# Block-sparse attention with a gated projection: the second half's keys in twelve smaller loads, and two more row loads in place of copies

## The chip, the cores and the metric

The kernel runs on one core of one Trainium2 chip. The metric is the time of one execution on the device in microseconds (us); the figure for a kernel is the median of its runs. Lower is better.

## The reference, cut to what matters

```python
# q, k, v: 4 batches, 8 heads, 768 rows, 64 columns; sampled_blocks: 24 x 3 block numbers
scores = scale * np.matmul(q, k.transpose(0, 1, 3, 2))
mask = np.abs(blk_i - blk_j) <= 1                      # blocks of 32 rows: own block and neighbours
mask = mask | (blk_i == 0) | (blk_j == 0) | (blk_i == 23) | (blk_j == 23)
for qb in range(24):
    for kb in sampled_blocks[qb]:                      # three sampled key blocks a query block
        mask[qb*32:(qb+1)*32, kb*32:(kb+1)*32] = True
attn = softmax(np.where(mask, scores, -1e9))
x = matmul(attn, v)                                    # heads joined: 4 x 768 x 512
gate_pre = causal depthwise convolution of x, 5 taps
out = (sigmoid(gate_pre) * (x @ w_val)) @ w_out
```

## The kernel before, in words

The four batches are worked off in two phases of two batches each (phase 0: batches 0 and 1, phase 1: batches 2 and 3). In a phase there are 22 ordinary parts, one for each query block `i` from 1 to 22, which serve both batches and all heads at once, and two global parts (query blocks 0 and 23 of one batch each, against all 24 key blocks), so 24 parts a phase. A global part takes two steps of the main loop (line 804), an ordinary part one. A step issues for its own part the score matmuls (tile `sc`, or `s` for a global part), for the part of the step before the transposes of the softmax weights (`pt`, evicted as `ptr`), for the part two steps before the products with the values (`av`). Around them it places pieces of the gate, the splitting of fp32 numbers into two parts, and the two projections (`vp`, `op`). Two tables of digits say how many such pieces each half step gets (lines 54 to 67). The order on each engine is fixed when the program is built.

The ordinary parts go in pairs (`PAIRS`: blocks 1 and 2, 3 and 4, and so on). Pair number `p` has the blocks 2p+1 and 2p+2.

**Keys.** The tile `keys` (`k` in the profile) holds one phase's keys of both batches, 24 blocks. `load_all_keys` (line 287) brings them in by `KEY_PARTS`; `K_AT` (line 34) names the part of the 48 with whose loads each piece is issued on SyncE's queue (SP). The phase 1 keys overwrite those of phase 0 block by block. For each pair `copy_keys` gathers the blocks that the pair needs into `kg`, a ring of two buffers of a pair each: the fixed blocks always by copies on GpSimd (POOL), and the three sampled blocks of a part by POOL copies out of `keys` (phase 0, blocks up to 18) or by SP loads from memory (all later ones, 128 KB each).

**Values.** A part needs the rows of its sampled blocks (`vb`, an indirect load of 128 rows which POOL issues, ring of three) and 128 rows for the fixed blocks: 64 end rows (blocks 0 and 23) and 64 own rows of the pair. For a pair of phase 0 with an even number `p`, the own rows lie in the upper half of a tile `vn` already, and the end rows are brought into its lower half; with an odd one the own rows are brought to the end rows in the tile `va`. They are brought by a POOL copy (`owns.append(copy_rows)`), or, for pairs from `ROWS_FROM` on, by a load of 260 KB on SP:

```python
            if f == 0 and pr.p >= ROWS_FROM:
                at, row = (2 * BLK, 2 * BLK * (pr.p + 1)) if own else (0, 0)
                sp.dma_start(pr.va[at : at + 2 * BLK]..., v[row : row + 2 * BLK, :])
            else:
                owns.append(copy_rows)
```

**Queues.** SP issues nearly all transfers in one order: queries (`qc`, ring of five), weights (`wst`), keys, sampled keys, rows and results. A transfer whose buffer is still read holds up those behind it. Each transfer also takes one of eight completion semaphores in turn, so SP waits for the transfer eight before it. POOL issues the indirect loads in order with its copies.

Of the kernel before, what the change touches and what calls it, by code (L numbers as in the profile page):

```python
# [17 lines left out]
BLK, NB, NR = 32, 24, 3  # L18
# [8 lines left out]
F, E = 2, B // 2  # L27
# [2 lines left out]
VRING = 3  # L30
GLOB_AT = ((0, 0), (12, 18))
V_AT = ((0, 0, 1, 1, 1, 1, 2, 2, 3, 4, 4, 5), (0, 0, 3, 12, 12, 16))
KEY_PARTS = (((0, 0, 8), (0, 8, 16), (0, 16, 24), (1, 0, 8), (1, 8, 16), (1, 16, 24)), tuple((E, a, a + 4) for a in range(0, NB, 4)))
K_AT = (0, 0, 0, 1, 1, 1, 22, 24, 24, 24, 27, 29)
LAG_T, LAG_V, LAG_X = 1, 2, 3
WEIGHTS_AT = (1, 2, 5, 6, 7, 8, 8, 9, 10, 11, 11, 12, 13, 14, 18, 19)
DECODE_LAG = 2
# [2 lines left out]
VALUES_FROM = 4  # L40
INDEX_AT = 3
SPARE_UNTIL = 18
ROWS_FROM = 4
WARM = 13
EVICTED = (4,)

# [25 lines left out]
def attention_moe(ctx, tc, qb, kb, v, sampled, w_val, conv_w, w_out, ident_in, slot_in, out):  # L72
# [210 lines left out]
    def load_all_keys():  # L283
        for f in range(F):
            for e, a, z in KEY_PARTS[f]:
                some = slice(e, e + 1) if e < E else slice(0, E)
# [59 lines left out]
    def load_keys(pr):  # L346
# [6 lines left out]
        if not pr.glob:  # L353
            for place, reg in block_numbers(pr, SP):
                sp.dma_start(pr.kg[:, 1 + pr.j, place], kb[:, f, :, bass.ds(reg, 1)].rearrange("p e o x -> p e (o x)"))
        for _ in range(K_AT.count(parts.index(pr))):
            next(loading_keys)
# [38 lines left out]
    def load_values(pr):  # L396
# [5 lines left out]
        if pr.j == 0:  # L402
# [17 lines left out]

            if f == 0 and pr.p >= ROWS_FROM:
                at, row = (2 * BLK, 2 * BLK * (pr.p + 1)) if own else (0, 0)
# [508 lines left out]
```

## Time and profile before

| | us |
|---|---|
| median of 3 runs | 353.4 (352.46 to 356.05) |
| profiled execution, its own time | 353.03 |
| span of the profile (first to last instruction) | 351.3 |
| TensorE matmul busy | 329.3 (94%) |
| VectorE busy | 274.9 (78%) |
| ScalarE busy | 226.3 (64%) |
| GpSimd busy | 118.7 (34%) |
| moved by DMA | 67.74 MB, mean 193 GB/s |

The profile is of one execution. PE is TensorE's matmuls, PEld its weight loads, DVE VectorE, ACT ScalarE, POOL GpSimd, SP SyncE's queue. Nearly all instructions pass through one recording helper, so they have line 90 (`L90`) and are told apart by their tiles. The idle time in brackets behind an instruction is that of its engine just before it, with what ended it; "issue" there means that the engine waited for nothing that the profile shows. The DMA share is the mean busy share of 16 DMA engines; it can go above 1, since the times of packets overlap.

### The profile page before, as it was taken

What the parts mean: (1) busy time and instruction counts of PE and PEld (TensorE: products, weight loads), DVE (VectorE), ACT (ScalarE), POOL (GpSimd) and SP (SyncE); (2) the same over time, 40 slices, a digit from 0 to 9 for tenths busy, and PEclk for the clock granted to TensorE, in tenths of its full rate; (3) what the DMA queues carried; (4) which work ended last, traced back from release to release, by engine and by line L of the source; (5) the groups of instructions that cost most, each with busy time, mean ns of one, the idle gap of its engine ahead of it and who ended that gap; (6) DMA issues with size and microseconds to landing.
All of it is one profiled execution on the core that took longest, in us unless ns stands there. A gap on an engine that the chain in (4) does not pass through costs nothing.

```text
span 351.3 us, 15356 instructions
## 1 busy us (share of the span) xinstructions
PE 329.3 (94%) x6522; PEld 258.0 (73%) x6522; DVE 274.9 (78%) x644; ACT 226.3 (64%) x505; POOL 118.7 (34%) x186
## 2 busy tenths in 40 slices
PE   8787989989867999999999999999999999999995
PEld 7465756655545887797788777887778878989894
DVE  0664878999999789759997984768987599989440
ACT  2365877687896757756785674758766786564421
POOL 1647788877643304414431222321242100000000
PEclk9899999999999999999999999999999999999999
DMA  6958587876999999774888567538663011020202
GB/s 219 395 194 261 174 266 256 276 251 170 277 283 294 385 247 305 250 225 154 273 228 279 165 205 219 173 107 251 200 204 95 12 58 62 30 90 2 90 0 90
DMA packets 47603, 67.74 MB, mean 193 GB/s; under 512 B 4400, under 2 KB 31536, under 8 KB 47536
## 3 DMA queue, kind: packets, MB, share of 16 engines
q1 hardware_dynamic: 40624, 43.10, 39.5%
q0 software_dynamic: 6336, 23.43, 21.1%
q8 instruction: 51, 0.84, 1.0%
q10 hardware_dynamic: 576, 0.24, 0.2%
q14 instruction: 16, 0.13, 0.1%
HBM read 60.46 MB, written 6.29 MB: 190 GB/s over the span
## 4 chain that ended last, share of the span: by engine, by line
PE 75%; DVE 14%; ACT 7%; issue 3%; POOL 0%; ACTq 0%; POOLq 0%; DVEq 0%
PE op L90 19%; PE vp L90 19%; PE av L90 12%; PE pt L90 11%; PE sc L90 9%; DVE mx L90 5%; PE s L90 3%; DVE words L90 3%; ACT ptr L90 3%; PE idle L90 2%; ACT pe L90 2%; DVE wst L90 2%; DVE xT L90 1%; DVE x L90 1%; DVE wv L90 1%
## 5 line engine op out<-in xcount | busy, mean ns | idle before, releaser
L90 ACT ACTIVATE pe<-sc,mx 128x256 f32<-128x256 f32 x176 | 69.1, 475 | 36.6 <-DVE mx L90 36.2
L90 POOL DMA_INDIRECT vb<-in_v,idx x44 | 44.4, 1010 | 142.7 <-PE av L90 120.8
L90 DVE SCALAR_TENSOR_TENSOR th<-xT,cw,th 128x384 f32<-128x384 f32 x128 | 79.7, 652 | 1.5 <-ACT th L90 1.5
L90 DVE TENSOR_REDUCE mx<-sc 128x2 f32<-128x512 f32 x88 | 56.3, 679 | 21.2 <-PE sc L90 17.5
L90 ACT COPY ptr<-pt 128x512 f32<-128x512 f32 x108 | 61.3, 606 | 9.3 <-PE pt L90 8.0
L90 POOL COPY kg<-k 128x256 f32 (+1 forms) x99 | 55.2, 596 | 7.5 <-PE sc L90 7.0
L90 PE MATMUL sc<-kg,qc 64*32 64x256 f32 x1408 | 53.3, 382 | 2.3 <-issue 1.1
L90 PE MATMUL op<-wo,yh 128*128 128x512 f32 x192 | 53.3, 399 | 0.0
L90 PE MATMUL pt<-ident,pe 128*128 128x128 f32 x352 | 50.4, 279 | 1.8 <-issue 1.8
L90 PE MATMUL vp<-xh,wv 128*128 128x384 f32 x256 | 51.1, 341 | 0.0
L90 PEld LDWEIGHTS vp<-xh,wv 128*128 128x128 f32 x256 | 44.3, 188 | 0.3
L90 PEld LDWEIGHTS pt<-ident,pe 128*128 128x128 f32 x352 | 38.5, 140 | 7.3 <-issue 1.9
L90 PEld LDWEIGHTS op<-wo,yh 128*128 128x128 f32 x192 | 35.3, 188 | 7.3
L90 PEld LDWEIGHTS sc<-kg,qc 64*32 64x32 f32 x1408 | 22.8, 106 | 21.2 <-issue 9.6
L90 ACT CAST yh<-y 128x384 fp32r<-128x384 f32 x32 | 16.8, 524 | 23.0 <-DVE y L90 23.0
L90 PE MATMUL av<-vb,ptr 128*32 128x65 f32 x1408 | 28.8, 220 | 2.4 <-issue 2.4
L90 PE MATMUL op<-wo,yl 128*128 128x512 f32 x96 | 30.9, 403 | 0.0
L90 PEld LDWEIGHTS av<-vn,ptr 128*32 128x32 f32 x1216 | 19.2, 109 | 14.6 <-ACT ptr L90 7.5
L90 PEld LDWEIGHTS av<-va,ptr 128*32 128x32 f32 x960 | 15.6, 109 | 17.2 <-ACT ptr L90 9.5
L90 PE MATMUL av<-vn,ptr 128*32 128x65 f32 x1216 | 24.5, 222 | 3.6 <-ACT ptr L90 1.7
L90 PE MATMUL vp<-xl,wv 128*128 128x384 f32 x128 | 27.7, 338 | 0.0
L90 DVE TENSOR_TENSOR yl<-y,yh 128x384 fp32r<-128x384 f32 x32 | 18.3, 572 | 11.4 <-ACT yh L90 11.1
(74 smaller groups left out, 421.8 us busy)
## 6 DMA issues: line engine op xcount, KB each, us to landing
kg<-in_k SPq DMA_DIRECT2D x80, 128.0 KB
qc<-in_q SPq DMA_DIRECT2D x48, 128.0 KB
k<-in_k SPq DMA_DIRECT2D x12, 512.0 KB
out<-ot SPq DMA_DIRECT2D x23, 256.0 KB
vn<-in_v SPq DMA_DIRECT2D x16, 260.0 KB
vn<-in_v SPq DMA_DIRECT2D x6, 520.0 KB
va<-in_v SPq DMA_DIRECT2D x8, 260.0 KB
wst<-in_w_val SPq DMA_DIRECT2D x8, 256.0 KB
```

The source lines that it names most:

```text
L90: made = getattr(self.eng, name)(*args, **kwargs)
```

## The change

Two edits of constants. The phase 1 keys come in twelve loads of two blocks (256 KB) in place of six of four blocks (512 KB), one each with the parts 21 to 32, where it was 22, three with 24, then 27 and 29. And `ROWS_FROM` goes from 4 to 2, so pairs 2 and 3 of phase 0 also load their 64 rows on SP, and POOL no longer copies them.

```diff
-KEY_PARTS = ((...), tuple((E, a, a + 4) for a in range(0, NB, 4)))
-K_AT = (0, 0, 0, 1, 1, 1, 22, 24, 24, 24, 27, 29)
+KEY_PARTS = ((...), tuple((E, a, a + 2) for a in range(0, NB, 2)))
+K_AT = (0, 0, 0, 1, 1, 1, 21, 22, 23, 24, 25, 26, 27, 28, 29, 30, 31, 32)
-ROWS_FROM = 4
+ROWS_FROM = 2
```

POOL, pair 3 of phase 0, around the indirect load of its first part (`vb_1186`, which is `vb_1187` in the change). Before:

```order
L90 DMA vb_1186<-in_v,idx_109 128x1040
L90 COPY va1_114<-vn_141 64x1040
L90 COPY kg0_111<-k_110 128x512
L90 COPY kg0_111<-k_110 128x2x256
L335 TENSOR_LOAD sm_103
```

The change:

```order
L90 DMA vb_1187<-in_v,idx_109 128x1040
L90 COPY kg0_111<-k_110 128x512
L90 COPY kg0_111<-k_110 128x2x256
L335 TENSOR_LOAD sm_103
```

The copy is gone and the key copies stand one place further ahead; the copy `vn_133<-vn_131` of pair 2 goes in the same way. No instruction moves on PE, DVE or ACT.

SP at the same stretch (`wst` are pieces of the weights, `qc` queries). Before:

```order
L90 DMA wst_907<-in_w_val 128x512
L90 DMA qc_1002<-in_q 128x256
L90 DMA wst_907<-in_w_val 128x512
L90 DMA wst_1006<-in_w_val 128x512
L90 DMA qc_1109<-in_q 128x256
L90 DMA wst_1006<-in_w_val 128x512
L90 DMA qc_1206<-in_q 128x256
```

The change:

```order
L90 DMA wst_907<-in_w_val 128x512
L90 DMA vn_133<-in_v 64x1040
L90 DMA qc_1002<-in_q 128x256
L90 DMA wst_907<-in_w_val 128x512
L90 DMA wst_1006<-in_w_val 128x512
L90 DMA qc_1109<-in_q 128x256
L90 DMA wst_1006<-in_w_val 128x512
L90 DMA va1_114<-in_v 64x1040
L90 DMA qc_1206<-in_q 128x256
```

Two row loads come in, the first ahead of `qc_1002`, the second ahead of `qc_1206`.

SP at the burst of key loads, with part 24 (`kg1_112` are its sampled keys). Before:

```order
L90 DMA kg1_112<-in_k 128x2x128
L90 DMA k_110<-in_k 128x2x512 x3
L90 DMA qc_2576<-in_q 128x256
L90 DMA vn_2578<-in_v 128x1040
```

The change:

```order
L90 DMA kg1_112<-in_k 128x2x128
L90 DMA k_110<-in_k 128x2x256
L90 DMA qc_2576<-in_q 128x256
L90 DMA vn_2578<-in_v 128x1040
```

Of 1,536 KB in a row 256 KB are left here. One load of 256 KB now stands behind the sampled keys of each of the parts 21 to 32.

## Rows read from the trace of the kernel before

**Rows 1.** The page: engines, the instruction queue, the chain by engine.

```profile
PE 329.3 (94%) x6522; PEld 258.0 (73%) x6522; DVE 274.9 (78%) x644; ACT 226.3 (64%) x505; POOL 118.7 (34%) x186
...
q8 instruction: 51, 0.84, 1.0%
...
PE 75%; DVE 14%; ACT 7%; issue 3%; POOL 0%; ACTq 0%; POOLq 0%; DVEq 0%
```

**Rows 2.** Stretches: window, length, busy by engine (instructions), clock, DMA share, GB/s.

```profile
40.00:46.00 6.00, 5.88 (x200) 4.50 (x200) 5.63 (x15) 5.01 (x14) 3.65 (x6) 1.00 0.60 171
46.00:52.00 6.00, 4.77 (x172) 3.14 (x156) 3.76 (x9) 4.19 (x10) 5.35 (x9) 1.00 0.82 274
...
97.00:103.00 6.00, 4.14 (x135) 2.80 (x119) 6.00 (x16) 5.13 (x14) 2.92 (x3) 1.00 1.09 270
103.00:109.00 6.00, 4.22 (x159) 2.97 (x147) 6.00 (x15) 5.28 (x13) 2.70 (x3) 1.00 0.97 279
...
115.00:121.00 6.00, 6.00 (x70) 5.21 (x72) 3.81 (x11) 5.21 (x12) 2.48 (x3) 1.00 1.05 395
121.00:127.00 6.00, 6.00 (x97) 5.87 (x97) 5.04 (x12) 4.12 (x10) 0.96 (x1) 1.00 1.13 243
```

**Rows 3.** Waits over the span: engine and tile, releaser, us, times, longest.

```profile
POOL vb L90 <- PE av L90: 120.8, 36, 11.4
...
PEld sc L90 <- POOL kg L90: 0.9, 3, 0.4
```

**Rows 4.** Waits of SP's queue over the span.

```profile
SPq L90 <- DMA k<-in_k: 7.0, 7, 1.5
```

**Rows 5.** Timeline of POOL: start, length, instruction, idle before it.

```profile
45.89 1.06 POOL L90 COPY vn<-vn 64x1040 f32<-64x1040 f32 x1
...
54.96 1.04 POOL L90 COPY va<-vn 64x1040 f32<-64x1040 f32 x1
...
116.33 1.17 POOL L90 COPY kg<-k 128x512 f32<-128x512 f32 x2
```

**Rows 6.** Timeline of SP's queue.

```profile
40.68 1.04 SPq L90 DMA_DIRECT2D wst<-in_w_val  x1
...
51.65 0.33 SPq L90 DMA_DIRECT2D qc<-in_q  x1
...
95.85 1.02 SPq L90 DMA_DIRECT2D qc<-in_q  x1
...
100.68 0.38 SPq L90 DMA_DIRECT2D k<-in_k  x1
...
110.28 2.52 SPq L90 DMA_DIRECT2D k<-in_k  x3
```

**Rows 7.** Timeline of PE, two stretches in which it pauses.

```profile
48.65 0.33 PE L90 MATMUL av<-va,ptr 128*32 128x65 f32 x9 [0.95 <-issue]
...
51.41 0.67 PE L90 MATMUL av<-va,ptr 128*32 128x65 f32 x32
...
53.17 0.50 PE L90 MATMUL av<-vb,ptr 128*32 128x65 f32 x18 [0.87 <-issue]
...
56.07 0.32 PE L90 MATMUL av<-vn,ptr 128*32 128x65 f32 x8
...
100.75 0.55 PE L90 MATMUL av<-vb,ptr 128*32 128x65 f32 x23 [1.57 <-issue]
...
106.30 1.09 PE L90 MATMUL pt<-ident,pe 128*128 128x128 f32 x8 [1.77 <-issue]
...
112.61 1.05 PE L90 MATMUL sc<-kg,qc 64*32 64x256 f32 x19 [0.89 <-issue]
```

**Rows 8.** Timelines: first uses of pair 3's rows (PE) and block 11's queries (ACT).

```profile
63.08 0.96 PE L90 MATMUL av<-va,ptr 128*32 128x65 f32 x32
...
64.61 0.41 ACT L90 ACTIVATE qc<-qc 128x256 f32<-128x256 f32 x1
```

**Rows 9.** The tile vb: its indirect loads, issue to landing.

```profile
DMA to landing us min/median/max: 5.0/5.8/8.0
```

More of the change, by code (lines that the diff above doesn't have):

```diff
@@ L32 @@
 V_AT = ((0, 0, 1, 1, 1, 1, 2, 2, 3, 4, 4, 5), (0, 0, 3, 12, 12, 16))
-KEY_PARTS = (((0, 0, 8), (0, 8, 16), (0, 16, 24), (1, 0, 8), (1, 8, 16), (1, 16, 24)), tuple((E, a, a + 4) for a in range(0, NB, 4)))
-K_AT = (0, 0, 0, 1, 1, 1, 22, 24, 24, 24, 27, 29)
+KEY_PARTS = (((0, 0, 8), (0, 8, 16), (0, 16, 24), (1, 0, 8), (1, 8, 16), (1, 16, 24)), tuple((E, a, a + 2) for a in range(0, NB, 2)))
+K_AT = (0, 0, 0, 1, 1, 1, 21, 22, 23, 24, 25, 26, 27, 28, 29, 30, 31, 32)
 LAG_T, LAG_V, LAG_X = 1, 2, 3
```

## The prediction

> **What bounds the kernel now.** I read first the page's engine line and its chain by engine: PE's matmuls are busy for 94% of the span, and 75% of the chain that ended last is PE's, 14% VectorE's, none POOL's [rows 1]. So a change of loads and POOL copies can only move the time where PE, or VectorE in its stead, waits for what it changes. Where that can be is in the table of stretches. From 115 us on PE is busy all of each stretch (6.00 of 6.00), while VectorE and POOL have gaps; there a transfer that comes earlier is worth nothing. Before, PE has gaps (4.14 and 4.22 of 6.00 in the two stretches from 97 to 109 us), and VectorE has none in these [rows 2]. The list of waits then says who would feel a faster POOL: POOL waits 120.8 us for PE to free the ring of `vb`, and the other way round PE's weight loads wait 0.9 us in all for POOL's key copies [rows 3]. Last, PE's timeline shows what its gaps are. The long ones are not waits for a tile at all: five pauses of 0.95, 0.87, 1.57, 1.77 and 0.89 us, marked as "issue", four of them in the middle of a group of equal matmuls whose first members had run [rows 7]. The page has a DMA queue for instructions, 51 packets and 0.84 MB [rows 1]; divided by PE's 13,044 instructions that is 64 bytes each, so this queue feeds PE, some 256 instructions a packet. I read the pauses as PE running out of instructions. The first two fall in or beside a stretch in which the DMA share has risen from 0.60 to 0.82, the others where it is 0.97 and more [rows 2]. So the load on the DMA engines is the one way in which this change can reach PE, and it matters from about 40 to 113 us.
>
> **The rows, part by part.** The change removes two POOL copies, 1.06 and 1.04 us [rows 5], and with them 2.1 us of POOL's time. Behind them wait the key copies of pairs 2 and 3, and behind those PE's score matmuls; that wait is at most the 0.9 us of the list, which three places share [rows 3]. I take nothing: from there to 109 us VectorE is full [rows 2] and its work is not shortened. Bounds: 0 and -0.5 us.
>
> In their place SP issues two loads of 260 KB. The first stands behind a piece of the weights issued by 41.7 us; its rows are first read at 56.07 us [rows 6, 7]. No row gives the landing time of such a load, but an indirect one of twice its size lands in 5.0 to 8.0 us [rows 9]. Even with 8.0 us it is there by 50. The second overwrites rows that pair 1 reads at 51.41 us for 0.67 us [rows 7], so it can only go out at 52.1 us, and SP waits there. Behind it are the queries of block 11, issued at 51.65 us so far [rows 6], and pieces of the weights. The queries go out some 0.5 us behind the load, at 52.6 us, and with 8.0 us land at 60.6; ScalarE first reads them at 64.61 us. The rows themselves land by 60.1, and PE reads them at 63.08 us [rows 8]. So both waits are covered, by 4.0 and 3.0 us. If that cover were gone (a landing of over 11 us), PE would wait for the rows next.
>
> The Trainium skill, "SBUF — State Buffer", section "SBUF: two separate sides", has VectorE and GpSimd lock one another out for a whole instruction on the port pair that they share, so by it each copy could hold up one VectorE instruction by its whole length and the change would give back up to 2.1 us. The list of waits above shows no VectorE work released by these copies, and the sum by the trace stays at 0.
>
> **The keys, part by part.** The bytes stay the same, 3 MB; SP issues six transfers more. One of 512 KB took SP 0.38 us, three in a row 2.52 us [rows 6], so 0.4 to 0.8 us each, 2.4 to 5 us spread over the steps from 95 us on. SP waits in that time for buffers that PE frees; I take 0. The first piece goes out behind the sampled keys of part 21, at about 96 us, the second where a load of 512 KB stood, at 100.7 us, the fourth at 110.3 us where now 1,536 KB go out [rows 6]. POOL's copy for the first pair of phase 1 starts at 116.33 us [rows 5], 15 us after the second piece, which it needs. Each later pair needs one piece more, while one goes out with every part, two for each pair. So no copy should wait for its keys.
>
> What is left is the effect on PE's pauses. Until 110 us there are now three pieces, 768 KB, where 512 KB stood: 256 KB more, which at the 279 GB/s of that stretch [rows 2] are 0.92 us of transfer. Behind 110 us there are 1,280 KB less, but from there PE has one pause left, 0.89 us, and its packet was probably under way by then. Bounds for the three pauses from 100 to 113 us: all gone, -4.23 us; each longer by the whole transfer, +2.8 us. I take +0.2 us: the two pauses ahead of the burst a little longer, the third shorter by half.
>
> The Trainium skill, "Runtime: NRT & Kernel Launch", section "Instruction fetch mechanics", says that the sequencer fetches the next 16 KiB of instructions while it runs the current ones and that the cost of crossing a block is mostly hidden. By that rule the term would be 0 whatever the DMA engines do. The five pauses speak against it here, as far as my reading of them holds.
>
> **The sum.** Against the profiled execution's own time of 353.03 us: rows 0, keys on SP 0, pauses +0.2, which makes 353.2 us. The median of the runs shown is 353.4, 0.4 us above that execution; the runs spread over 3.6 us, 1%, so less than 1% can't be told from no change. I forecast no change.
>
> **The rivals.**
>
> 1. Faster: PE's instruction packets get through. For it: three pauses, 4.23 us, lie in the stretch with the highest DMA share, and the largest burst of the kernel, 1,536 KB in one go, is taken apart. Against it: two of the pauses lie ahead of the burst, and ahead of it the change adds bytes. If all three go, 353.4 - 4.2 = 349.2 us; with two of them, about 350.2.
>
> 2. Slower, in the same place: the stretch from 95 to 110 us gets 256 KB more while its DMA share is 0.97 to 1.09 already. Each pause then grows by up to 0.92 us, and the two at 48 and 53 us by as much, since the first row load falls ahead of them: five times 0.92 is 4.6 us, 358 us; the three late ones alone 356.2. It decides from the point at which the share in 97 to 109 us stays above about 1.1. Against it: at 115 to 121 us the engines moved 395 GB/s at a share of 1.05, so 270 and 279 GB/s are not all that they can do [rows 2].
>
> 3. Slower: the smaller key loads are moved at the worse of two rates. At 243 GB/s, the rate from 121 to 127 us, 3.1 MB take 12.8 us, at 395 GB/s 8.0 [rows 2]. If these 4.8 us came on the path, 358.2 us. But only SP has waited for keys until now, 7.0 us in all [rows 4], and the cover is 15 us, so a copy on POOL would have to come that late before it decides. The Trainium skill, "DMA: Bandwidth & Descriptors", section "Measured (HBM→SBUF, 128 partitions, SWDGE, issued from GpSimd)", asks for transfers of 1 MiB and more, which speaks against splitting; its figures are for another path, and no run here shows a load alone.
>
> 4. The change does little because its parts never were on the path: that is the forecast itself. That it doesn't do what it says I rule out by the order of instructions: both copies are gone, the burst is one load.
>
> **How the numbers follow.** The forecast gets 0.74, rival 1 0.13, rival 2 0.10, rival 3 0.03. The forecast's own range is 352.2 to 354.5 us, from the bounds of the small terms and half of one pause either way. Rivals 1 and 2 reach over 1% (below 349.9 or above 356.9) only when most of their pauses go or grow. Faster by over 1%: 0.08 from rival 1 and 0.02 for what I don't see. Slower by over 1%: 0.06 from rival 2, 0.03 from rival 3 and 0.01 for what I don't see. Within 1%: 0.80. The range runs from 350.0, two pauses gone and a little more, to 355.8 us, the three late pauses longer by most of their bound.
>
> **What would show it.** In the profile after: no POOL copy of 64 rows at 46 and 55 us and key copies 1 us earlier there, with PE's first 115 us no shorter than by 0.5 us; a row load on SP at about 52 us with the queries right behind it; key loads of one each from about 96 us to 170 us; PE full from 115 us on. I would be wrong if PE or POOL waited for `k`, `va` or `vn`, or if the sum of the pauses marked "issue" between 45 and 113 us, 6.05 us now [rows 7], changed by more than 2 us.

## The result: 0.6 to 1.5% slower, and the profile after

The changed kernel takes 355.67 us (median of 5 runs, 354.46 to 359.62); the kernel before took 353.4 beside it (median of 5). The ratio is 1.0102, with an interval of 1.0056 to 1.0149. Each ratio here is taken over the undisturbed executions and is not the plain quotient of two medians, which is 1.0064 in this case. The forecast was 353.2 us and no change. The time is inside the range, at its upper end, but the forecast's case is wrong: the change costs about 1%.

The profiled execution of after took 354.46 us, 1.4 us more than that of before; it is the fastest of its five. The page answers to [rows 1]:

```profile
span 352.7 us, 15365 instructions
PE 328.0 (93%) x6522; PEld 257.5 (73%) x6522; DVE 276.2 (78%) x644; ACT 226.2 (64%) x505; POOL 118.3 (34%) x184
...
q8 instruction: 51, 0.84, 1.0%
```

Two POOL instructions are gone (184 for 186), and no engine in this line has more instructions than before (VectorE is busy for 1.3 us more, PE for 1.3 us less). So I looked for the loss in the waiting. The table of stretches answers to [rows 2], with a stretch that I had not asked for before, 52 to 58 us, and two more at the end:

```profile
40.00:46.00 6.00, 5.66 (x156) 3.86 (x158) 5.12 (x15) 5.65 (x15) 5.02 (x9) 1.00 0.82 216
46.00:52.00 6.00, 4.03 (x142) 2.91 (x143) 4.10 (x10) 3.46 (x9) 3.81 (x7) 1.00 0.89 287
52.00:58.00 6.00, 4.51 (x127) 3.21 (x126) 5.00 (x16) 4.87 (x14) 4.54 (x8) 1.00 0.88 268
...
97.00:103.00 6.00, 5.21 (x147) 3.61 (x136) 6.00 (x14) 5.05 (x13) 3.10 (x4) 1.00 1.11 267
103.00:109.00 6.00, 4.43 (x111) 2.76 (x110) 6.00 (x17) 5.45 (x14) 1.31 (x2) 1.00 0.97 297
...
121.00:127.00 6.00, 6.00 (x121) 5.37 (x121) 3.85 (x10) 4.91 (x13) 1.35 (x1) 1.00 1.11 284
66.02:69.44 3.42, 3.42 (x72) 2.93 (x61) 3.05 (x8) 2.15 (x5) 1.52 (x2) 0.50 0.59 209
13.70:17.15 3.45, 1.94 (x31) 1.30 (x16) 2.97 (x8) 2.34 (x6) 3.00 (x13) 1.00 1.05 390
```

The same view of the kernel before, for the two stretches that its rows lack:

```profile
52.00:58.00 6.00, 4.85 (x149) 3.47 (x138) 5.09 (x13) 4.96 (x13) 5.20 (x9) 1.00 0.72 240
13.73:17.15 3.42, 3.42 (x38) 2.08 (x23) 1.94 (x6) 1.51 (x5) 2.96 (x13) 0.50 1.06 394
```

Read the DMA share, second from the end. From 40 to 58 us it was 0.60, 0.82 and 0.72, and is now 0.82, 0.89 and 0.88; PE's busy time falls from 4.77 to 4.03 us in the second of these stretches and from 4.85 to 4.51 in the third. From 97 to 109 us, where I had placed most of the risk, PE is busier than before (5.21 and 4.43 for 4.14 and 4.22). And in after the granted clock was 0.50 (1.2 GHz in place of 2.4) from 66.02 to 69.44 us, where before had 1.00.

PE's timeline says what the gaps are; it answers to [rows 7]:

```profile
47.81 0.33 PE L90 MATMUL av<-va,ptr 128*32 128x65 f32 x9 [1.43 <-issue]
...
52.88 0.50 PE L90 MATMUL av<-vb,ptr 128*32 128x65 f32 x18 [1.42 <-issue]
...
58.58 0.55 PE L90 MATMUL pt<-ident,pe 128*128 128x128 f32 x3 [1.16 <-issue]
...
65.22 0.66 PE L90 MATMUL sc<-kg,qc 64*32 64x256 f32 x13 [2.02 <-issue]
...
101.80 0.55 PE L90 MATMUL av<-vb,ptr 128*32 128x65 f32 x24 [0.51 <-issue]
...
107.78 0.24 PE L90 MATMUL av<-vb,ptr 128*32 128x65 f32 x1 [1.29 <-issue]
```

The first two are the pauses of 0.95 and 0.87 us in [rows 7], in front of the same matmuls; they have grown to 1.43 and 1.42. At 58 and 65 us there are two that before did not have, 1.16 and 2.02 us, and the stretch at half clock begins right behind the second. So the long pauses between 45 and 70 us went from 1.82 to 6.03 us in these two traces, and those from 97 us on from 4.23 to 1.80.

They don't stand at chance places. Between the pauses at 47.81, 52.88, 58.58 and 65.22 us PE's timeline has 127, 127 and 126 matmuls, each with its weight load, so some 254 instructions. That is close to the 256 instructions a packet that the prediction worked out from the instruction queue [rows 1]. Before's two lie 127 matmuls apart too, and in e1 those at 63.77 and 69.76 us 126; between before's at 53.17 and 100.75 us lie 1,139, which is nine times 126.6. So each kernel pauses at some of the same places in the program.

How this adds up is seen by laying the same groups of matmuls side by side. In PE's timeline of before:

```profile
32.42 1.18 PE L90 MATMUL av<-vn,ptr 128*32 128x65 f32 x65 [0.44 <-issue]
33.53 1.09 PE L90 MATMUL pt<-ident,first 128*128 128x128 f32 x8
...
40.08 0.67 PE L90 MATMUL av<-vn,ptr 128*32 128x65 f32 x32
...
68.87 1.09 PE L90 MATMUL pt<-ident,pe 128*128 128x128 f32 x8
```

In that of after, the same three groups and the pause between the first two:

```profile
30.17 1.09 PE L90 MATMUL pt<-ident,first 128*128 128x128 f32 x8
...
37.77 1.06 PE L90 MATMUL sc<-kg,qc 64*32 64x256 f32 x23 [1.44 <-issue]
38.76 0.67 PE L90 MATMUL av<-vn,ptr 128*32 128x65 f32 x32
...
71.54 1.09 PE L90 MATMUL pt<-ident,pe 128*128 128x128 f32 x8
```

After was 1.1 us ahead at 9 us and still at 28 us, so before's stretch at half clock near its start (13.73 to 17.15 us, above; after's had none) had cost it nothing by then. At the first of the three groups it is 3.4 us ahead, since before loses 2.3 us around three short pauses of 0.42 to 0.45 us. At the second it is 1.3 us ahead, since after loses 2.0 us around its pause at 37.77 us, which lies ahead of the first row load (40.40 us) and so isn't the loads'. At the third it is 2.7 us behind. So some 4.0 us were lost from 40 to 70 us, and the pauses there are 4.2 us longer; the half clock behind the last of them adds to that (4.0 us behind at 69.46 us), but before then waits 1.00 us for the softmax, and little of it is left. Behind 97 us the pauses are 2.4 us shorter, and after ended 1.4 us behind. Such sums hold for one pair of executions; the ratio over the runs is the better measure of the loss.

The rest went as the prediction had it. SP's timeline after answers to [rows 6]:

```profile
40.40 0.56 SPq L90 DMA_DIRECT2D vn<-in_v  x1
...
51.30 0.47 SPq L90 DMA_DIRECT2D va<-in_v  x1
51.87 0.53 SPq L90 DMA_DIRECT2D qc<-in_q  x1
...
97.68 0.89 SPq L90 DMA_DIRECT2D k<-in_k  x1
...
109.52 1.44 SPq L90 DMA_DIRECT2D k<-in_k  x1
```

The second row load goes out at 51.30 us with the queries right behind it, and no engine waits for either. The waits answer to [rows 3] and [rows 4]:

```profile
POOL vb L90 <- PE av L90: 114.6, 35, 11.4
...
PEld sc L90 <- POOL kg L90: 0.7, 3, 0.4
...
SPq L90 <- DMA k<-in_k: 4.5, 5, 1.1
```

### The profile page after: what moved, and what is told of

Same layout as the page of the kernel before. It is cut to its first block, busy times and chain, and to the rows that moved or that the text cites. A ratio compares the mean times of both kernels' runs of the same rounds, so it can differ in the third digit from the quotient of the medians.

```text
span 352.7 us, 15365 instructions
## 1 busy us (share of the span) xinstructions
PE 328.0 (93%) x6522; PEld 257.5 (73%) x6522; DVE 276.2 (78%) x644; ACT 226.2 (64%) x505; POOL 118.3 (34%) x184
## 4 chain that ended last, share of the span: by engine, by line
PE 73%; DVE 13%; DMA 6%; ACT 4%; issue 3%; SPq 0%; ACTq 0%; DVEq 0%
PE op L90 19%; PE vp L90 18%; PE av L90 13%; PE pt L90 11%; PE sc L90 10%; DMA vn<-in_v 4%; DVE mx L90 3%; PE s L90 2%; DVE th L90 2%; ACT ptr L90 2%; ACT pe L90 2%; DVE words L90 2%; DVE wst L90 1%; DMA k<-in_k 1%; DVE xT L90 1%
## 5 line engine op out<-in xcount | busy, mean ns | idle before, releaser
L90 POOL COPY kg<-k 128x256 f32 (+1 forms) x99 | 57.6, 618 | 7.5 <-PE sc L90 7.0
L90 PE MATMUL pt<-ident,pe 128*128 128x128 f32 x352 | 51.4, 283 | 1.2 <-issue 1.2
L90 PE MATMUL av<-vb,ptr 128*32 128x65 f32 x1408 | 29.7, 222 | 3.3 <-issue 3.2
L90 PEld LDWEIGHTS av<-vb,ptr 128*32 128x32 f32 x1408 | 24.2, 111 | 4.0 <-issue 3.9
```

Of the source, the lines that this page charges most:

```text
L90: made = getattr(self.eng, name)(*args, **kwargs)
```

## The experiments

Three theories stood against each other.

- **A, traffic.** The 520 KB of the two row loads fall into 40 to 60 us. There they hold up the packets that bring PE its instructions; PE pauses longer and more often, and what it loses grows by a fall of the granted clock. Nothing needs to wait for the loads.
- **B, keys.** The twelve key loads do it.
- **C, order.** The copies that left POOL, or SP's wait in front of the second load, shift the work of some engine. The traffic is harmless.

Each experiment ran beside the kernel before. All edits are to the kernel before unless it is said otherwise. "Clock" is the granted clock as a mean over a kernel's runs (e8's without one execution of 515.69 us); the runs of before had 0.992 to 0.995, those of after 0.984.

| experiment | ratio to before | clock |
|---|---|---|
| e1 rows alone | 1.0095 [1.0055, 1.0136] | 0.987 |
| e2 keys alone | 1.0001 [0.9966, 1.0036] | 0.995 |
| e3 copies kept, two loads that nobody needs | 1.0127 [1.0087, 1.0167] | 0.989 |
| e4 neither copies nor loads | 0.9982 [0.9946, 1.0019] | 0.994 |
| e5 four such loads | 1.0110 [1.0053, 1.0168] | 0.983 |
| e6 two such loads at 129 us | 1.0005 [0.9972, 1.0039] | 0.992 |
| e7 all pairs by copies | 1.0136 [1.0093, 1.0180] | 0.989 |
| e8 loads from pair 6 on | 1.0022 [0.9989, 1.0055] | 0.990 |
| e9 rows, fewer weights | 1.0036 [0.9994, 1.0079] | 0.991 |
| e10 before, fewer weights | 1.0018 [0.9982, 1.0053] | 0.992 |
| e11 first row load alone | 1.0067 [1.0036, 1.0099] | 0.989 |
| e12 second row load alone | 1.0106 [1.0058, 1.0154] | 0.991 |
| e13 two loads of 128 rows x 2,080 bytes | 1.0048 [1.0010, 1.0086] | 0.992 |
| e14 two loads of half the bytes | 1.0052 [1.0015, 1.0088] | 0.988 |
| e15 two loads at 65 and 83 us | 1.0062 [1.0028, 1.0097] | 0.990 |

### The two halves of the change: e1 and e2

```diff
-ROWS_FROM = 4
+ROWS_FROM = 2        (e1; KEY_PARTS and K_AT as before)
```

> ROWS_FROM = 2 alone, keys as before. Theory A (the two row loads put 520 KB of traffic into 40 to 60 us, PE's instruction packets come later, its pauses there grow, and after a long one the granted clock falls): ratio 1.008 to 1.013, the whole of the loss; the sum of PE's long 'issue' pauses from 45 to 70 us about 6 us in place of 1.8, mean clock lower than before's in most runs. Theory B (the loss is the key pieces): ratio 0.998 to 1.002. Theory C (POOL's copies shifted to collide with VectorE): ratio about 1.01 too, but with VectorE's instructions longer, not PE's pauses.

```diff
-KEY_PARTS = (..., tuple((E, a, a + 4) for a in range(0, NB, 4)))
-K_AT = (0, 0, 0, 1, 1, 1, 22, 24, 24, 24, 27, 29)
+KEY_PARTS = (..., tuple((E, a, a + 2) for a in range(0, NB, 2)))
+K_AT = (0, 0, 0, 1, 1, 1, 21, 22, 23, ..., 31, 32)     (e2; ROWS_FROM = 4)
```

> Twelve key pieces alone, ROWS_FROM = 4. Theory A: nothing changes before 95 us, and the pauses from 95 to 115 us shrink or stay: ratio 0.992 to 1.002. Theory B: ratio 1.008 to 1.013 with longer pauses from 95 to 170 us.

The rows carry all of the loss, the keys none, so B is out. In e1 PE's timeline has a pause in front of the same matmuls as before and after, now of 2.37 us:

```profile
48.96 0.33 PE L90 MATMUL av<-va,ptr 128*32 128x65 f32 x9 [2.37 <-issue]
...
69.76 0.49 PE L90 MATMUL av<-va,ptr 128*32 128x65 f32 x20 [1.64 <-issue]
```

and its granted clock was 0.50 behind both, in these stretches, and in a third from 101.5 to 104.9 us, behind a pause of 1.37 us:

```profile
50.30:53.70 3.40, 3.40 (x69) 1.84 (x71) 3.37 (x9) 2.11 (x4) 3.25 (x4) 0.50 0.50 157
70.80:74.20 3.40, 3.40 (x40) 2.08 (x40) 3.38 (x5) 2.54 (x7) 3.14 (x6) 0.50 0.63 166
```

PE is busy for all of the 3.40 us there, and yet does 69 and 40 matmuls: a busy share says nothing of the rate. The long pauses from 45 to 70 us sum to 4.82 us, where some 6 were expected. In e2 the late pauses are 0.99 and 0.74 us where [rows 7] has 1.57, 1.77 and 0.89:

```profile
98.82 0.55 PE L90 MATMUL av<-vb,ptr 128*32 128x65 f32 x23 [0.99 <-issue]
...
111.13 1.05 PE L90 MATMUL sc<-kg,qc 64*32 64x256 f32 x19 [0.74 <-issue]
```

The twelve loads may ease those, but e2's pauses at 67 and 77 us (0.71 and 1.24 us) are new, and the ratio shows no gain.

### Copies or loads: e3 and e4

e3 keeps the two copies, and so the order on POOL, and adds two loads of the same size and form at the same places. They go into the tile `va0`, which no pair of phase 0 uses, into rows that are overwritten before they are read; no engine needs them.

```diff
             else:
                 owns.append(copy_rows)
+                if f == 0 and pr.p >= 2:
+                    at, row = (2 * BLK, 2 * BLK * (pr.p + 1)) if own else (0, 0)
+                    sp.dma_start(va[0][at : at + 2 * BLK]..., v[row : row + 2 * BLK, :])
```

> The kernel before with both POOL copies kept, and the same two loads of 260 KB issued at the same places into a tile that nothing reads in this phase, so that only the traffic is added. Theory A: as slow as the rows alone, ratio 1.008 to 1.013, pauses on PE between 45 and 70 us. Theory C or a wait for late rows: ratio 0.998 to 1.003, since no engine waits for these loads and POOL's order is that of before.

```diff
-            else:
+            elif f or pr.p < 2:          (e4)
```

> The kernel before without the two POOL copies and without loads in their place: the 64 rows of pairs 2 and 3 of phase 0 are left as they stand in the tile (other values, same work). Theory A: like before or a little faster, ratio 0.995 to 1.001. Theory C (earlier key copies on POOL cost): ratio 1.005 or more.

This pair decides between A and C. Traffic alone, with the copies in their place, costs 1.27%; taking the copies away without the traffic changes nothing. The second load of e3 goes out at 47.33 us, so SP's wait for the tile, until 51.30 in after, isn't needed for the loss either:

```profile
41.00 0.75 SPq L90 DMA_DIRECT2D va<-in_v  x1
...
47.33 0.47 SPq L90 DMA_DIRECT2D va<-in_v  x1
```

Nor did other data come late: between 40 and 115 us no engine but SP's queue waits for a transfer in the traces of after and e5, and in those of e1 and e3 PE's weight loads do so once, 0.2 us, for sampled keys. So the loads themselves cost the time, and not a wait for what they bring.

How they cost it, the traces show less well. The profiled executions of e1 and e3 (353.72 and 353.61 us) are the fastest of their 12 and only some 0.6 us above that of before, so most of the loss isn't in them. And the long pauses from 45 to 70 us sum to 3.39 us in e3, but to 2.80 in e4 and 3.57 in e6, which are no slower than before. PE's timeline and the stretches of e3 show the chain that A has, at one place: a pause of 1.42 us, then half clock, and eight transposes that take 1.97 us where eight take 1.09 at 106.30 us in [rows 7]:

```profile
48.14 0.33 PE L90 MATMUL av<-va,ptr 128*32 128x65 f32 x9 [1.42 <-issue]
...
49.23 1.97 PE L90 MATMUL pt<-ident,pe 128*128 128x128 f32 x8
```

```profile
46.00:52.00 6.00, 4.42 (x96) 3.31 (x96) 3.75 (x10) 3.30 (x8) 4.46 (x8) 0.72 1.04 299
48.40:51.80 3.40, 3.40 (x61) 2.67 (x58) 2.43 (x7) 1.09 (x2) 2.22 (x3) 0.50 1.06 311
```

### How much, and where: e5, e6 and e15

e5 is e3 with two loads at each place. e6 puts e3's two loads at 129 us, where PE has no gaps. e15 puts two ahead of the row loads of pairs 5 and 7; in its trace they go out at 64.79 and 83.09 us.

```diff
+                if f == 0 and pr.p >= 2:                     (e5)
+                    for at in (0, 2 * BLK):
+                        row = 2 * BLK * (pr.p + 1) if at else 0
+                        sp.dma_start(va[0][at : at + 2 * BLK]..., v[row : row + 2 * BLK, :])
```

> The kernel before with four loads of 260 KB that nothing reads, two at each of the two places, copies kept: twice the added traffic. Theory A (traffic from 40 to 60 us starves PE of instructions, its clock falls): ratio 1.015 to 1.03, above that of two such loads (1.0127), mean granted clock in the runs below 0.989. If a load costs only by where it stands in SP's queue, whatever it moves: about 1.013 again.

```diff
+            if f and pr.p == 0:                              (e6)
+                for at in (0, 2 * BLK):
+                    sp.dma_start(va[0][at : at + 2 * BLK]..., v[at : at + 2 * BLK, :])
```

> The kernel before with two loads of 260 KB that nothing reads, issued with the first part of phase 1 (about 125 us), where PE is full of projection matmuls. Theory A: these matmuls are long, PE has no pauses there, so ratio 0.997 to 1.004 and a clock like before's. If any 520 KB more costs about 1%: 1.008 to 1.013.

```diff
+            if f == 0 and pr.p in (5, 7):                    (e15)
+                sp.dma_start(va[0][32 * (pr.p - 5) : 32 * (pr.p - 5) + 64]..., v[0:64, :])
```

> Two loads of 260 KB (64 rows of 4,160 bytes) that nothing reads, beside the row loads of pairs 5 and 7, at about 68 and 85 us, where VectorE is full and PE waits for it in every step. Theory A: PE has time to spare there, ratio 0.999 to 1.005. If 520 KB anywhere before 113 us cost the same: 1.009 to 1.013.

e6 met A's expectation: the same bytes cost nothing at 129 us, though the DMA share there is 0.97.

```profile
126.00:132.00 6.00, 6.00 (x116) 4.48 (x115) 5.88 (x17) 3.09 (x8) 0.00 (x0) 1.00 0.97 271
```

PE does 116 matmuls in these 6 us, all of them busy, where before it does 172 and 149 in the stretches at 46 and 52 us. That PE takes in fewer instructions there fits A; no run shows that this is why the loads do no harm.

e5 and e15 missed A's expectation. Twice the traffic had longer pauses in its profile, in PE's timeline of e5:

```profile
49.20 0.33 PE L90 MATMUL av<-va,ptr 128*32 128x65 f32 x9 [2.52 <-issue]
...
66.94 0.72 PE L90 MATMUL sc<-kg,qc 64*32 64x256 f32 x13 [1.99 <-issue]
...
110.52 1.09 PE L90 MATMUL pt<-ident,pe 128*128 128x128 f32 x8 [2.93 <-issue]
```

but the time was not longer: 1.0110 for e3's 1.0127, with wide intervals. That is what e5's other reading expected, a load that costs by its place in SP's queue, whatever it moves; e14 (below) speaks against it, not clear of its interval. And in e15 the loads cost 0.6%, where A as I had put it expected at most 0.5. So the loss doesn't grow in proportion to the bytes, and the harmful part of the program is not 40 to 60 us alone; loads at 41 to 83 us cost, at 129 us they do not.

### Less traffic: e7 to e10

e7 and e8 go the other way: copies for all pairs, or for all up to 5.

```diff
-ROWS_FROM = 4
+ROWS_FROM = 12       (e7; 6 in e8)
```

> The change turned round: ROWS_FROM = 12, no row loads in phase 0 at all, seven loads of 260 KB fewer than before (from 57 to 113 us) and seven POOL copies more. Theory A: ratio 0.990 to 1.000, fewer long pauses from 57 to 113 us, clock above before's 0.995. If POOL's time counts more than the traffic (its key copies come late, or its copies lock VectorE out): ratio 1.003 to 1.02.

> ROWS_FROM = 6: the loads at about 57 and 68 us become POOL copies again, the five later ones stay. Theory A: ratio 0.993 to 1.000. If POOL counts more: 1.002 to 1.01.

e7 is the run that shows most. Its traffic in 57 to 113 us fell, from a DMA share of 0.88 to 0.72, and every long "issue" pause there is gone (the one at 48 us, 1.43 us, is left). And yet it is 1.4% slower, with a clock of 0.989, where A expected it faster and the clock above 0.995. The stretch of e7, its waits there and VectorE's groups there:

```profile
57.00:113.00 56.00, 45.88 (x1308) 30.45 (x1299) 55.69 (x117) 41.45 (x100) 40.81 (x61) 1.00 0.72 221
```

```profile
PEld sc L90 <- ACT pe L90: 9.4, 8, 2.5
PEld sc L90 <- issue: 1.8, 11, 0.2
```

```profile
L90 DVE SCALAR_TENSOR_TENSOR th<-xT,cw,th 128x384 f32<-128x384 f32 x11 | 8.3, 773 | 0.0
```

The same three views of the kernel before:

```profile
57.00:113.00 56.00, 47.27 (x1325) 31.28 (x1315) 55.69 (x124) 44.09 (x106) 37.13 (x56) 1.00 0.88 256
```

```profile
PEld sc L90 <- issue: 4.7, 16, 1.4
PEld sc L90 <- ACT pe L90: 3.2, 4, 1.5
```

```profile
L90 DVE SCALAR_TENSOR_TENSOR th<-xT,cw,th 128x384 f32<-128x384 f32 x13 | 7.9, 628 | 0.0
```

VectorE is full in both (55.69 us), but does 117 instructions in e7 and 124 before; the operation that sums the gate's convolution (`th`) takes 773 ns in place of 628, and 617 to 644 in every other kernel here. So with copies POOL is in VectorE's way, as I read it, and PE then waits for the softmax, whose maxima VectorE finds (6.2 us more of `ACT pe`), in place of its instructions. The Trainium skill, "SBUF — State Buffer", section "SBUF: two separate sides", says that a GpSimd instruction and a VectorE operation with two SBUF inputs, as `th` is, lock each other out of the port pair that they share; e7's 773 ns agree with it.

So both ways of bringing the rows have a price, and it looks as if which is higher depends on who is full. From 57 us on VectorE is the full one, and loads are the better way for the seven pairs together; the copies at 45.89 and 54.96 us [rows 5] lie where VectorE has gaps, 3.76 and 5.09 of 6.00 us busy, and cost nothing there (e4). e8, with pairs 4 and 5 as copies too, can't be told from before, so the price of a single copy behind 57 us is open.

e9 makes the change's rows with two pieces of the weights left out, e10 leaves out the same two alone.

```diff
+            if n in (4, 5):
+                yield
+                staged.append((step[0], staged[n - 4][1]))
+                yield
+                continue          (e9, with ROWS_FROM = 2; e10 without)
```

> The rows alone (ROWS_FROM = 2), but pieces 4 and 5 of the weights are not loaded (1 MB less, due at 52 to 61 us; the pieces 0 and 1 are decoded a second time in their place, so the work is the same and the output is not). Theory A: traffic taken away beside the row loads gives back most of the loss: ratio 0.996 to 1.004, clock 0.991 or more. If the loss hangs on the row loads themselves (their place in SP's queue, their buffers): ratio 1.007 to 1.013.

> The kernel before with the same two pieces of the weights not loaded (same work, another output). Theory A: less traffic than before in 52 to 61 us, so ratio 0.990 to 0.999. If traffic is no matter there: 0.999 to 1.002.

e9's loss is 0.36%, for e1's 0.95%: with less of the other traffic, some 60% of the loss is gone. The intervals of the two overlap, so this supports A without proving it. e10 gains nothing, where A expected up to 1%: the traffic that before has anyway is not worth taking away.

### One load, and its form: e11 to e14

```diff
-            if f == 0 and pr.p >= ROWS_FROM:
+            if f == 0 and pr.p >= ROWS_FROM and pr.p != 3:    (e11; != 2 in e12; ROWS_FROM = 2)
```

> Only pair 2's rows are loaded (at about 41 us), pair 3's are copied by POOL as before. Theory A, in parts: half of the traffic, half or more of the loss, ratio 1.003 to 1.010. If the loss comes from SP waiting at the second load (pair 3's, 52 us): 0.998 to 1.002.

> Only pair 3's rows are loaded (at about 52 us). Theory A, in parts: ratio 1.002 to 1.007. If the loss comes from SP waiting at this load: 1.008 to 1.013.

```diff
+                if f == 0 and pr.p >= 2:
+                    sp.dma_start(va[0][:, pr.p - 2], v[0:128, 0 : H * DV])                           (e13)
+                    sp.dma_start(va[0][64 * (pr.p - 2) : 64 * (pr.p - 1), 0], v[0:64, 0 : H * DV])   (e14)
```

> The kernel before with two loads of 260 KB that nothing reads at the two places, as in the run with copies and loads, but shaped 128 rows of 2,080 bytes and not 64 rows of 4,160. If the bytes count: ratio 1.007 to 1.013 as there. If it was the long packets on half of the partitions that hold up PE's instructions: 0.999 to 1.004.

> The same two loads with half of the bytes, 64 rows of 2,080 (130 KB each). If the bytes count, about half of the loss: ratio 1.003 to 1.008. If any load at these places costs the same: 1.009 to 1.013. If only the long packets count: 0.999 to 1.003.

Either row load alone costs already (1.0067 and 1.0106), and both together no more than the second (1.0095): again no sum, as in e5. e12's figure is the least sure: it is of six runs, from 350.97 to 357.55 us, and lies in the range that its expectation gave to SP's wait; e11, which has no such wait, and e3 speak against that. With the same 260 KB as 128 rows of 2,080 bytes in place of 64 rows of 4,160, or with half of the bytes, some 40% of e3's loss is left (1.0048 and 1.0052), with intervals that end where e3's begins. The runs don't tell whether the bytes, the length of a row or the number of partitions counts most.

## Why the prediction was wrong, point by point

- **Where the bound is: right.** The load on the DMA engines is the way in which this change reached the time; the copies and the keys have no part that shows (e4, e2). "It matters from about 40 to 113 us" holds as far as it was tried: loads at 41 to 83 us cost (e1, e3, e15), at 129 us they do not (e6).
- **The rows: the step that failed.** "I take nothing ... Bounds: 0 and -0.5 us" prices the two loads by their landing and by the time that POOL saves. Both came out: nothing waits for the rows or the queries, and the copies were worth nothing (e4: 0.9982). One reason given for the second was misread, though: VectorE isn't full "from there to 109 us", it is busy for 3.76 and 5.09 of 6.00 us in the stretches of the two copies. But the 520 KB of traffic have no term in this step. By e3 that term is as large as the whole result: +1.27% [0.87, 1.67], 3.1 to 5.9 us of the 353.0. I had written down the way from traffic to PE, and then used it only for the 256 KB of the keys, in the later stretch.
- **The keys: right.** Taken as 0 on SP and +0.2 us in the pauses; e2 has 1.0001 [0.9966, 1.0036], and no copy waited for its keys. POOL did wait once, 4.89 us ahead of an indirect load at 145.34 us, for what the trace puts down to a key load, which was named as a sign of being wrong; PE is busy for 6.00 of 6.00 us there, and e2 shows no price. The pauses from 97 us on shrank by 2.4 us in after's trace, which is neither of the bounds; in the time it does not show.
- **Rival 2** had the mechanism and the two pauses at 48 and 53 us, but its weight on the wrong end of the program. Its price of up to 0.92 us a pause was enough for these (0.48 and 0.55 longer); it lacked the two pauses that came new (3.18 us together) and the clock. By the distances above, a pause that isn't in the trace of before can come at any of the places that lie some 127 matmuls apart. Its point of decision, a DMA share above 1.1 in 97 to 109 us, was at the wrong place: at 40 to 58 us 0.82 to 0.89 was enough.
- **The clock** had no place in the prediction. Over 85 runs of the kernel before (those beside e1 to e12), time and granted clock go together (correlation -0.69; a straight line gives 351.3 us at full clock and 2.4 us more for each 0.01 less). e1's clock is 0.0082 lower than that of before beside it, by this line some 2.0 us of its mean 3.0; the rest would be the pauses themselves. This is a correlation: no experiment set the clock alone, and it doesn't order the kernels by itself: e9 and e12 both have 0.991, with 1.0036 and 1.0106. What PE did before each fall in the three traces shown here is a long pause for instructions: 2.02 us (after), 2.37, 1.64 and 1.37 (e1), 1.42 (e3). But not every such pause has a fall behind it: after's 1.43 and 1.42 us and one of 2.16 us in e7 have none. And e6, no slower than before, has a fall near 100 us behind a pause of 1.52 us.
- **What would show it.** I had said that I would be wrong if the sum of the pauses between 45 and 113 us changed by more than 2 us. It went from 6.05 to 7.83 us, 1.78 more, and I was wrong all the same: the sum hides that 4.2 came in front and 2.4 went behind, and it holds nothing of the clock.
- **The page on instructions.** The Trainium skill, "Runtime: NRT & Kernel Launch", section "Instruction fetch mechanics", has the fetch of the next block mostly hidden. The traces differ: pauses of up to 2.4 us stand in the middle of groups of equal matmuls (after, e1, e3). That these are instruction fetches is inferred, from the word "issue", from the queue of 51 packets, and above all from their distance of some 254 instructions or a multiple of it; no row of the trace shows a packet and the pause that it ends side by side.

What stays open: how the loads' cost comes about in the runs that show it, since the pauses and the clock are read from single executions; how much of the loss is the clock's, why it does not add up (e5, e11, e12), and which property of a load counts (e13, e14). No version beat both kernels. The kernel before with its copies for pairs 2 and 3 stays the best of those that do all of the work; e2 and e8 can't be told from it.

## What to carry to other kernels

A load that nobody waits for isn't always free, here at 41 to 83 us, where PE runs many short matmuls: give its traffic a term of its own, against PE's instruction supply, in the stretch where it is moved, before asking when it lands. Whether a copy on GpSimd or a load brings a tile is asked stretch by stretch: here copies cost nothing where VectorE has gaps, and seven of them cost 1.4% where it is full. And when a mechanism has been found in the profile, it has to be put to every part of the change, not only to the part in which it was first seen.

## What the runs showed that was not expected

- The price of traffic is not in proportion to its bytes: 260 KB more cost 0.67 or 1.06% (e11, e12), 520 KB 0.95 and 1.27 (e1, e3), 1,040 KB 1.10 (e5), all with overlapping intervals.
- The same load at a DMA share of 0.97 costs nothing where PE runs 116 matmuls in 6 us (e6, 1.0005).
- The pauses keep to places: 126 or 127 matmuls with their weight loads lie between neighbours (after, 47.81 to 65.22 us), which is about one packet of instructions; at which of them it pauses differs from trace to trace, also between kernels that are equally fast (before, e4, e6).
- Two traces of kernels that run the same instructions on PE were 3.4 us apart at 33 us and 1.3 us apart at 40 us, ahead of anything that the change moves, by pauses at different places. That is as much as the whole effect. Traces have to be laid side by side from the start, group by group, or such a lead is taken for an effect.
